# Attention layers on Trainium2: a third buffer for residual rows, weight loads spread over the steps, mask copies placed first

## The chip, the cores and the metric

The kernel runs on one NeuronCore of a Trainium2 chip. The metric is the device time of one execution, in microseconds (us). Three runs of the kernel before took 1181.93, 1186.46 and 1187.51 us; their median is 1186.46. One further execution was recorded by the hardware profiler; its durations are the ones used below. Engine names are those of the profile: PE is TensorE (matmuls), DVE is VectorE, ACT is ScalarE, POOL is GpSimd, SP is SyncE, which here only issues DMAs. A line L540 is line 540 of the kernel before.

## The reference

Four layers run one after the other on a bf16 input x of 2048 rows by 576 columns: A, B, A, B. Each adds its result to x, and each works on the LayerNorm of x.

```python
def _A_ref(x, wqkv, wo):          # H = 32, Dh = 18, W = 8, dil = 2
    qkv = transpose((x @ wqkv).reshape(B, S, 3, H, Dh), 2, 0, 3, 1, 4)
    q, k, v = (qkv[0], qkv[1], qkv[2])
    idx = arange(S)[:, None] - (arange(W) * dil)[None, :]
    ...
    logits = einsum('bhsd,bhswd->bhsw', q, kg) * Dh ** (-0.5)   # kg, vg: rows idx of k and v
    attn = softmax(where(idx >= 0, logits, -1e9))
    o = einsum('bhsw,bhswd->bhsd', attn, vg)
    return transpose(o, 0, 2, 1, 3).reshape(B, S, D) @ wo

def _B_ref(x, w_in, w_sp, b_sp, w_out):   # F = 4608, Fh = 2304
    z = gelu(einsum('bsd,df->bsf', x, w_in))
    z1, z2 = z[..., :Fh], layernorm(z[..., Fh:])
    g = einsum('ts,bsf->btf', w_sp, z2) + b_sp[None, :, None]
    return einsum('bsf,fd->bsd', z1 * g, w_out)

x = x + _A_ref(layernorm(x), ...); x = x + _B_ref(layernorm(x), ...)   # twice
```

So A is attention in which a row sees itself and seven earlier rows, two apart. B is a gated MLP whose gate mixes rows with a 2048 x 2048 matrix.

## The kernel before, in words

**Order of the work.** Layer A writes the order of its instructions out by hand for all engines (`tc.manual_schedule`): each engine runs its instructions in the order in which the program lists them, and waits where an operand is not ready. B does so for DVE and ACT in its first phase. SP and POOL also issue DMAs (L78); a DMA that must wait holds up whatever stands behind it on that engine.

**Layer A** (`layer_A`, L339) works on 17 tiles of rows in 34 steps, two steps per tile, one for each half of the heads. Step s holds the logits of step s+1 (`L_mm`, PE, L463), their exponential (`EXP`, ACT, L472), the product with v of step s (`PV`, PE L486, then the division into `o_t` on DVE, L492 and L493, and a transpose of `o_t` by DMA into `o_slot`), and then whatever `table[s]` lists. The table is filled with `at(step, function, ...)`:

- `PG` (L412): five matmuls (L428) project 512 columns of q or k into a PSUM bank; DVE (L397) or ACT copies them to a staging buffer `stg`; when both halves are staged, DMAs of 72 KB move each head's rows to their places in `QK`. These moves take the queues of their issuers in turn: `(sync, gpsimd)` by default, or `q2 = (gpsimd, sync, gpsimd)` (L561). Some PGs run ahead of step 0 (the list `pre`), others in steps 1 to 14.
- `VW`: the projection of v (L405).
- `O_CP`: DVE copies `o_slot` into the ring `oT` (L512). The last tiles are instead transposed by PE and copied by ACT (`O_T`, L518).
- `XO(i)` (L525): for even i, SP loads the residual rows i and i+1 of x into a buffer `xo` (288 KB in layer 0, 576 KB in layer 2; layer 0's are bf16, layer 2's float32). There are 2 such buffers.
- `WO(i, hh)` (L533): five matmuls (L540) of the output projection into a bank, and DVE adds `xo` to give `x_new` (L543). Row i's two halves stand at the steps `wo_steps[i]`: 8 and 9 for row 0, then about two steps later for each row, up to 34 and after for rows 14 and 15.
- `LN_STATS` (DVE statistics L234 and L236, POOL's reciprocal root L238 and L239), `LN_XN` (POOL, L259 and L262): the LayerNorm of `x_new` for layer B. `XST` and `XN_ST` store `x_new` and the normalised rows, `LN_T` loads the latter transposed into `xnT`, all through SP.

Ahead of step 0 in layer 0 stands a prologue: loads of x and weights, the LayerNorm of the 16 row tiles (`S_`, `R_`, `A_`, `T_`), the load of the mask pattern (`load_pat`), and `fill_window_rows(QK, 0)` (L194), which copies the mask rows into `QK` on DVE (L198 and L202) for one half of the columns. The heads' rows that the DMAs move land in the same tile `QK`, and the DMAs wait for these copies. In layer 2 the masks are copied after the first PGs, behind `setup_bufs` (DVE memsets of `P_sb` and `o_t`, L388 and L390) and the memset of `v_ext` (L687).

**Weights of the next layer.** B's z phase needs `win2a` (three chunks of 128 rows of `w_in`, loaded in 6 pieces of 288 KB) and `win2b` (6 pieces, into the room of the q/k weights). In layer 0 two of `win2a`'s three chunks are lent out as staging buffers until step 0's moves have gone; the third is not. For the second B layer `win2a` is loaded in the first one, by ACT (L1028); `win2b` is loaded in each A layer, by POOL.

**Layer B** (`layer_B`, L792) first makes z2 (z phase): groups of 8 units, each unit a PSUM bank of 128 x 512 (L851). ACT evicts them through GELU into `zp` (L898; 3 buffers, pool `p1`), DVE takes statistics (L900), DVE and POOL normalise into `Z`. Then come the gate (L975 for z1, L999 for the row mixing, the largest part) and the output (L1048, L1058).

**Pools.** A pool is a stretch of on-chip memory per partition, opened and closed with its layer. Layer A's small tiles (`x_new`, `xo`, `rec`, `ln_st`, `ln_mv`, `ln_rstd` and others) are in the pool `A{li}_sb` (L362). When a later pool takes the same bytes, the first instruction that writes a tile there waits for the last readers of the tiles that it covers (`reuse_waits="tile"`).

Of the kernel before, what the change touches and what calls it, by code (L numbers as in the profile page):

```python
# [13 lines left out]
bf16 = mybir.dt.bfloat16  # L14
# [4 lines left out]
P = 128  # L19
D = 576  # L20
# [43 lines left out]
class K:  # L64
# [274 lines left out]
    def layer_A(self, li):  # L339
        nc, tc, cfg = self.nc, self.tc, self.cfg  # L340
        S, NT, XW, NS = cfg.S, cfg.NT, cfg.XW, cfg.NS
        scale = float(DH ** -0.5)
        x_prev = self.A_x if li == 0 else self.xres[li - 1]
        x_prev_dt = bf16 if li == 0 else f32
# [6 lines left out]
        QK = main.tile([P, 2, 8, XW], bf16, name="QK")  # L351
# [10 lines left out]
        sb_cm = tc.tile_pool(name=f"A{li}_sb", bufs=2, reuse_waits="tile")  # L362
        sb = sb_cm.__enter__()
        x_news = [sb.tile([P, D], f32, name="x_new", tag="x_new", bufs=4) for k_ in range(4)]
        xos = {k_: sb.tile([P, 2, D], x_prev_dt, name="xo", tag="xo", bufs=2) for k_ in range(2)}
        if self.right is None:
            self.open_right()
        R = self.right
# [10 lines left out]
        def q0_(t):  # L379
            return cfg.tiles[t][0]  # L380
# [5 lines left out]
        def setup_bufs(eng):  # L386
            for pb in P_bufs:
                eng.memset(pb[:, :, :, QT:P], 1.0)  # L388
            for ob_ in o_bufs:
                eng.memset(ob_[:, D:640], 0.0)  # L390

        def exp_table():
            nc.scalar.activation(out=P_bufs[0][:, 0, 0, 0:1], in_=self.ones[:, 0:1], func=ACT.Exp)
# [130 lines left out]

        def XO(i):  # L525
            if i % 2 == 0:
                xo = xos.pop(i // 2, None) or sb.tile([P, 2, D], x_prev_dt, name="xo", tag="xo", bufs=2)
                src = self.rows_of(x_prev, i, 2) if li == 0 else x_prev[i * P:(i + 2) * P, :]
                self.dma(xo[:], src.rearrange("(a p) d -> p a d", p=P), eng=nc.sync)
                for k_ in range(2):  # L530
                    tails[i + k_] = dict(xo=xo[:, k_, :])
# [29 lines left out]
        q2 = (nc.gpsimd, nc.sync, nc.gpsimd)  # L561


        if li == 0:
# [32 lines left out]
            def S_(*tiles):  # L597
                for i in tiles:
                    st = sb.tile([P, 2, nc.vector.BN_STATS_DIM], f32, name="ln_st", tag="ln_st", bufs=3)
                    for s in range(2):  # L600
                        nc.vector.bn_stats(out=st[:, s, :], in_=xts[i][:, s * 288:(s + 1) * 288])
                    nc.vector.bn_aggr(out=mvs[:, i, :], in_=st[:])

            def R_(i0, n):
                rs = rstds[:, i0:i0 + n]
                nc.vector.tensor_scalar_add(out=rs, in0=mvs[:, i0:i0 + n, 1], scalar1=EPS)
                nc.gpsimd.tensor_tensor(out=rs, in0=rs, in1=self.neg_half[:, 0:1].to_broadcast([P, n]), op=ALU.pow)
            xns = {}

            def A_(*tiles):  # L610
                for i in tiles:
                    xns[i] = xn = self.xn_bufs[self.xn_rr % len(self.xn_bufs)]
                    self.xn_rr += 1
                    nc.vector.tensor_scalar(out=xn[:, 0:D], in0=xts[i], scalar1=mvs[:, i, 0:1],
                                            scalar2=rstds[:, i:i + 1], op0=ALU.subtract, op1=ALU.mult)
# [45 lines left out]
            self.load_pat(nc.sync)  # L661
            S_(9, 10, 11)
            R_(8, 4)
            S_(12)
            A_(8, 9, 10, 11)
            T_(8, 9, 10, 11)
# [14 lines left out]
        else:  # L681
            for k_, (d, cc) in enumerate([(d, cc) for d in range(5) for cc in range(2)]):
                for qk in ((1, 0) if d < 4 else (0,)):
                    PG(d, qk, cc, k_ == 0, (nc.gpsimd, nc.sync) if d == 0 else q2)
                if k_ == 0:
                    setup_bufs(nc.vector)
                    nc.vector.memset(v_ext[:, :, :, DH:DH + 1], 1.0)  # L687
                    self.fill_window_rows(QK, 0)
                    exp_table()
                if k_ == 1:  # L690
                    self.run_deferred()
                if k_ == 6:
                    self.fill_window_rows(QK, 1)
# [15 lines left out]
        def at(s, f, *a):  # L709
            table.setdefault(s, []).append((f, a))  # L710
        pgs = [(d, qk, cc) for d, cc in ((0, 2), (1, 2), (2, 2), (0, 3), (1, 3), (2, 3), (3, 2), (3, 3), (4, 2), (4, 3))
               for qk in ((1, 0) if d < 4 else (0,))]
        PG_END = 14
        pre, pgs = pgs[:6], pgs[6:]
        for k_, (d, qk, cc) in enumerate(pgs):
            at(1 + k_ if li == 0 else (k_ * PG_END) // len(pgs), PG, d, qk, cc, True)
        vws = [(t, hh) for t in range(nvw, NT) for hh in range(2)]
        if li == 0:
            at(0, VW, *vws[0], True)
# [10 lines left out]
        wo_steps = list(zip(units[0::2], units[1::2]))  # L730
        assert len(wo_steps) == NS
        for t in range(NT - 2):
            s = wo_steps[q0_(t) // P][0] - 1
            if t < NT - 3 and not in_ring(t):
                at(min(2 * t + 6, s), O_CP, t)
        for i in range(NS):
            s, s1 = wo_steps[i]
            if i % 2 == 0:
                at(max(s - 4, wo_steps[i - 3][1] + 1) if i >= 4 else s - 5, XO, i)
            at(s, WO, i, 0)  # L740
            at(s1, WO, i, 1)
            at(s1, LN_STATS, i)
            at(s1 + 1, LN_XN, i)
            at(s1 + 1, XST, i)
            if i < NS - 1:
                at(s1 + 4, XN_ST, i)
            if NS // 2 <= i < NS - 1:
                for k_ in range(2):
                    at(max(s1 + 6, NST + 3 * (i - NS // 2) - 4), LN_T, 2 * i - NS + k_)
        at(2 * (NT - 3) + 3, O_CP, NT - 3)  # L750
        if li == 0:
            at(0, self.load_wo, nc.sync)
            seen = sb.tile([P, 1], bf16, name="x_seen", tag="x_seen", bufs=1)
            at(0, lambda: nc.gpsimd.tensor_copy(out=seen[:], in_=self.xnT[:, 0, S - 1:S]))
            for f in reversed(self.load_win2a(nc.gpsimd)):
                at(0, f)
        at(PG_END + 1, alloc_win2b)
        for k_ in range(6):
            at(PG_END + 1 + k_, win2b_piece, k_)
        at(NST - 2, O_T, NT - 2)  # L760
        at(NST, O_T, NT - 1)
        for k_, (d, qk, cc) in enumerate(pre):
# [398 lines left out]
```

## Time and profile before

| what | value |
|---|---|
| median of three runs | 1186.46 us |
| the profiled execution: its own time | 1186.85 us |
| its span in the profile | 1185.1 us |
| PE busy | 1158.1 us, 98% |
| DVE, ACT, POOL busy | 47%, 29%, 24% |
| mean granted PE clock | 0.992 |
| layer 0 ends and its z phase starts at about | 134 us |
| layer 2 starts at about | 600 us, its z phase at 718 us |

"Busy" is the time in which an engine had an instruction running; PE's matmuls overlap, so a busy PE need not be at its peak. The granted clock is the share of full speed that the throttle left PE. A time line gives the start, the duration, the engine, line and operation, and in square brackets the idle time ahead of it with the instruction that released it. The chain of waits follows the work that ended last back from one instruction to what released it. For a DMA, "landing" is the time from its issue to its arrival.

### The profile page before, as it was taken

The numbers are of one execution on the slowest core, as the hardware profiler recorded it, in microseconds if no ns is written. First come the engines' busy times: TensorE is split into PE (matmuls) and PEld (weight loads), VectorE is DVE, ScalarE is ACT, GpSimd is POOL, SyncE is SP. The second block draws the span as 40 slices with busy tenths as digits, with TensorE's granted clock in tenths as the row PEclk, the third lists the DMA queues.
The fourth block names the chain that finished last, engine by engine and source line by source line (L and its number), as shares of the span: only waits on it lengthen the run. The fifth ranks groups of instructions, "written<-read, shape, count | busy, mean of one in ns | idle before, by whom it ended". The sixth has DMA issues, their size and how long they took to land.

```text
span 1185.1 us, 20051 instructions
## 1 busy us (share of the span) xinstructions
PE 1158.1 (98%) x8258; PEld 613.4 (52%) x8258; DVE 552.3 (47%) x1137; ACT 338.3 (29%) x491; POOL 280.9 (24%) x412
## 2 busy tenths in 40 slices
PE   9979899999999999999999998999999999999998
PEld 5547444444444444457755664444444444444677
DVE  8758688422233332245555785873232233232322
ACT  5559455111100111102147883550111110111000
POOL 3749855100000000001144796550000000000000
PEclk9989999999999999999999998999999999999999
DMA  8889796000000000049536798920000000001332
GB/s 194 186 145 252 191 210 142 23 12 12 12 1 12 12 12 1 18 142 283 170 85 122 190 257 198 230 67 13 12 12 12 12 1 12 12 1 37 116 106 73
DMA packets 182801, 106.44 MB, mean 90 GB/s; under 512 B 134939, under 2 KB 164043, under 8 KB 182710
## 3 DMA queue, kind: packets, MB, share of 16 engines
q1 hardware_dynamic: 170117, 84.54, 30.3%
q0 software_dynamic: 6240, 14.88, 4.7%
q10 hardware_dynamic: 6352, 5.75, 1.6%
q8 instruction: 64, 1.05, 0.4%
q14 instruction: 28, 0.22, 0.1%
HBM read 42.40 MB, written 21.77 MB: 54 GB/s over the span
## 4 chain that ended last, share of the span: by engine, by line
PE 90%; DMA 4%; DVE 3%; POOL 1%; ACT 1%; issue 1%; SPq 0%; DVEq 0%; POOLq 0%; ACTq 0%
PE pg L999 42%; PE po L1048 12%; PE pz L851 6%; PE pz L975 6%; PE pz1s L975 6%; PE pzs L851 6%; PE pp L428 4%; PE pv L405 2%; PE pw L540 2%; PE O_ps L486 2%; PE L_ps L463 1%; DMA QK<-stg 1%; DMA xo<-xres 1%; POOL QK L78 1%; ACT P_sb L472 1%
## 5 line engine op out<-in xcount | busy, mean ns | idle before, releaser
L999 PE MATMUL pg<-Wq,Z 128*128 128x512 bf16 x2304 | 500.2, 379 | 0.0
L999 PEld LDWEIGHTS <-Z 128*128 128x128 bf16 x2304 | 225.4, 98 | 271.8
L1003 DVE TENSOR_TENSOR g_tmp<-pg,ln_xn 128x512 f32<-128x512 f32 x144 | 99.6, 692 | 421.6 <-PE pg L999 421.6
L994 ACT ACTIVATE z1T<-pz 128x1024 bf16<-128x1024 f32 x36 | 34.9, 1020 | 500.2 <-PE pz L975 500.2
L78 POOL DMA_DIRECT2D wout<-in_B_w_out_dram x4 | 4.3, 1080 | 598.8 <-PE pg L999 598.8
L1048 PE MATMUL po<-wout,Z 128*128 128x288 bf16 x1152 | 141.4, 286 | 0.0
L472 ACT ACTIVATE P_sb<-L_ps 128x1440 bf16<-128x1440 f32 (+3 forms) x136 | 125.0, 972 | 36.8 <-PE L_ps L463 35.6
L1048 PEld LDWEIGHTS <-Z 128*128 128x128 bf16 x1152 | 112.7, 98 | 28.8
L851 PEld LDWEIGHTS <-xnT 128*128 128x128 bf16 (+1 forms) x800 | 68.9, 98 | 77.2 <-issue 12.5
L1004 DVE TENSOR_TENSOR Z<-g_tmp,z1T 128x512 bf16<-128x512 f32 x144 | 99.7, 692 | 12.2
L900 DVE BATCH_NORM_STATS2 z_st<-zp 128x6 f32<-128x512 bf16 (+1 forms) x160 | 91.7, 618 | 27.9 <-ACT zp L898 27.7
L975 PEld LDWEIGHTS <-w 128*128 128x128 bf16 (+1 forms) x640 | 53.7, 97 | 74.0 <-issue 13.6
L428 PE MATMUL pp<-xnT,wqk_sb 128*128 128x512 bf16 x360 | 83.6, 382 | 1.1 <-DVE o_t L493 1.1
L259 POOL TENSOR_SCALAR ln_xn<-x_new,ln_mv,ln_rstd 128x576 bf16<-128x576 f32 x32 | 74.1, 2314 | 2.3
L1058 DVE TENSOR_TENSOR x_new<-po,xo 128x288 f32<-128x288 f32 (+1 forms) x64 | 28.8, 455 | 87.4 <-PE po L1048 83.2
L975 PE MATMUL pz<-xnT,w 128*128 128x512 bf16 (+1 forms) x320 | 66.5, 380 | 0.0
L975 PE MATMUL pz1s<-xnT,w 128*128 128x512 bf16 (+1 forms) x320 | 66.5, 379 | 0.0
L540 PE MATMUL pw<-wo_sb,oT 128*128 128x288 bf16 x320 | 50.6, 296 | 13.9 <-DVE x_new L543 12.6
L851 PE MATMUL pz<-win2a,xnT 128*128 128x512 bf16 (+1 forms) x240 | 61.3, 367 | 0.0
L851 PE MATMUL pzs<-win2a,xnT 128*128 128x512 bf16 (+1 forms) x240 | 59.5, 358 | 0.0
L78 POOL DMA_DIRECT2D QK<-stg x80 | 48.6, 611 | 39.8 <-DVE stg L397 15.8
L898 ACT ACTIVATE zp<-pz 128x1024 bf16<-128x1024 f32 (+2 forms) x56 | 36.6, 720 | 74.4 <-PE pz L851 74.4
(108 smaller groups left out, 941.7 us busy)
## 6 DMA issues: line engine op xcount, KB each, us to landing
xres<-x_new SPq DMA_DIRECT2D x48, 288.0 KB
xo<-xres SPq DMA_DIRECT2D x32, 288.0 KB
wout<-in_B_w_out_dram POOLq DMA_DIRECT2D x4, 1296.0 KB, 7.5
xn_rows<-ln_xn SPq DMA_DIRECT2D x32, 160.0 KB
xo<-xres SPq DMA_DIRECT2D x8, 576.0 KB
w<-in_B_w_in_dram SPq DMA_DIRECT2D x16, 256.0 KB
QK<-stg POOLq DMA_DIRECT2D x52, 72.0 KB, 4.9
QK<-stg SPq DMA_DIRECT2D x42, 72.0 KB
```

What stands on the lines that cost most here:

```text
L78: return eng.dma_start(out=out, in_=in_)
L259: e.tensor_scalar(out=xn[:nrows, 0:D], in0=x_t[:nrows, :], scalar1=mv[:nrows, 0:1], scalar2=rstd[:nrows, 0:1], op0=ALU.subtract, op1=ALU.mult)
L428: nc.tensor.matmul(pp[:, :], lhsT=w, rhs=self.xnT[:, c, cc * 512:(cc + 1) * 512], start=(c == 0), stop=(c == 4))
L472: nc.scalar.activation(out=P_bufs[2 * jp + s % 2][:nk, :, :, 0:nq], in_=Lv[:nk, :, :, 0:nq], func=ACT.Exp, scale=scale)
L540: nc.tensor.matmul(pw[:, 0:288], lhsT=oT[:, c, r0:r0 + P], rhs=wo_sb[:, c, hh * 288:(hh + 1) * 288], start=(c == 0), stop=(c == 4))
L851: nc.tensor.matmul(out[:, o0:o0 + n], lhsT=self.xnT[r0:r1, c, r * P:(r + 1) * P], rhs=win2(c)[r0:r1, w0:w0 + n], start=start, stop=stop, t ...
L900: nc.vector.bn_stats(out=st[:, x // 512, :], in_=zp[:, x:x + min(512, w0 + n - x)])
L975: nc.tensor.matmul(outs[a_], lhsT=w1[r0:r1, c, sub * P:(sub + 1) * P], rhs=self.xnT[r0:r1, c, q * 512:(q + 1) * 512], start=start, stop=st ...
L999: nc.tensor.matmul(pg[:, :], lhsT=Z[:, jj, i, sub * P:(sub + 1) * P], rhs=Wq[q][:, i, :], start=(i == 0), stop=(i == NS - 1))
L1003: nc.vector.tensor_tensor(out=tmp[:], in0=pg[:, :], in1=bsp[:, qs], op=ALU.add)
L1004: nc.vector.tensor_tensor(out=uT(jj)[:, sub, qs], in0=tmp[:], in1=z1Ts[jj, sub][:, qs], op=ALU.mult)
L1048: nc.tensor.matmul(acc[hh], lhsT=u_rows(j, i), rhs=wouts[j // NJH][:, j % NJH, hh * 288:(hh + 1) * 288], start=(j == 0), stop=(j == NJ - 1))
```

## The change

- **Residual rows.** `xo` gets 3 buffers instead of 2 in both A layers, and the loads go out earlier. For i = 0, 2, ... 14 they stood at steps 3, 7, 12, 16, 19, 23, 27, 31 and now stand at 2, 6, 10, 12, 16, 20, 24, 27.
- **z weights.** All six pieces of `win2a` went out on POOL at step 0 of layer 0, behind a small copy (`x_seen`) that waited for the last transposed row. Now the two pieces of the chunk that is not lent go out on POOL in the prologue, after the statistics of row tiles 8 to 11; the other four go out at steps 13 to 16, by POOL and SP in turn. `x_seen` is gone.
- **win2b.** Its six pieces stood at steps 15 to 20 of both A layers and now stand at 17, 19, 21, 23, 25 and 27.
- **Moves.** In layer 0 the PGs of steps 1 to 8 use `q2`. With the order of the others this gives POOL 6, 5 and 5 of each group of eight moves and SP 2, 3 and 3, where each had 4.
- **Masks.** In layer 2 `fill_window_rows(QK, 0)` stands ahead of the memsets.

```diff
-        xos = {k_: sb.tile([P, 2, D], x_prev_dt, name="xo", tag="xo", bufs=2) for k_ in range(2)}
+        xos = {k_: sb.tile([P, 2, D], x_prev_dt, name="xo", tag="xo", bufs=3) for k_ in range(3)}
...
-                xo = xos.pop(i // 2, None) or sb.tile([P, 2, D], x_prev_dt, name="xo", tag="xo", bufs=2)
+                xo = xos.pop(i // 2, None) or sb.tile([P, 2, D], x_prev_dt, name="xo", tag="xo", bufs=3)
...
             R_(8, 4)
+            for f in self.load_win2a(nc.gpsimd)[4:6]:
+                f()
             S_(12)
...
                 if k_ == 0:
+                    self.fill_window_rows(QK, 0)
                     setup_bufs(nc.vector)
                     nc.vector.memset(v_ext[:, :, :, DH:DH + 1], 1.0)
-                    self.fill_window_rows(QK, 0)
                     exp_table()
...
-            at(1 + k_ if li == 0 else (k_ * PG_END) // len(pgs), PG, d, qk, cc, True)
+            at(1 + k_ if li == 0 else (k_ * PG_END) // len(pgs), PG, d, qk, cc, True, *((q2,) if li == 0 and k_ < 8 else ()))
...
-                at(max(s - 4, wo_steps[i - 3][1] + 1) if i >= 4 else s - 5, XO, i)
+                at(max(s - 7, wo_steps[i - 5][1] + 1) if i >= 6 else s - 6, XO, i)
...
-            seen = sb.tile([P, 1], bf16, name="x_seen", tag="x_seen", bufs=1)
-            at(0, lambda: nc.gpsimd.tensor_copy(out=seen[:], in_=self.xnT[:, 0, S - 1:S]))
-            for f in reversed(self.load_win2a(nc.gpsimd)):
-                at(0, f)
-        at(PG_END + 1, alloc_win2b)
+            for k_ in range(4):
+                at(PG_END - 1 + k_, self.load_win2a((nc.gpsimd, nc.sync)[k_ % 2])[k_])
+        s_b = PG_END + 3
+        at(s_b, alloc_win2b)
         for k_ in range(6):
-            at(PG_END + 1 + k_, win2b_piece, k_)
+            at(s_b + 2 * k_, win2b_piece, k_)
```

In the built program the third buffer moves the end of layer A's small pool. Before, it ended at byte 189,380 of a partition in layer 0 and 187,300 in layer 2, and the first buffer of `zp` in the next layer B began at 190,976. Now it ends at 191,652 and 191,908, so that some of its last tiles (`rec`, `ln_st`, `ln_mv`, `ln_rstd` among them) share bytes with that buffer.

## The prediction

> **What bounds it now.** I read the busy table, the chain of waits and the groups by cost, then the time line where TensorE (PE) idles.
>
> ```profile
> PE 1158.1 (98%) x8258; PEld 613.4 (52%) x8258; DVE 552.3 (47%) x1137; ACT 338.3 (29%) x491; POOL 280.9 (24%) x412
> L540 PE MATMUL pw<-wo_sb,oT 128*128 128x288 bf16 x320 | 50.6, 296 | 13.9 <-DVE x_new L543 12.6
> ```
>
> PE is busy 98%, so only its holes and its half-clock time can be won. The largest holes have one line, 12.6 us ahead of the output projection (L540), where PE waits for a bank that DVE's residual add (L543) must empty. I follow three of them and the start of layer 2.
>
> **Hole 1, layer 0, 72–77 us.** The chain from 45 to 85 us (start, us, what):
>
> ```profile
> 56.34 9.87 DMA QK<-stg
> ...
> 66.27 9.99 DMA o_slot<-o_t
> ...
> 77.05 1.36 PE pw L540 x5
> ```
>
> Two transfers of 10 us in a row end in PE's 4.03 us wait at 77.05. Why so slow? DMAs issued from 49 to 60 us (x, KB each, median us to landing):
>
> ```profile
> win2a<-in_B_w_in_dram POOLq DMA_DIRECT2D x6, 288.0 KB, 10.7
> QK<-stg POOLq DMA_DIRECT2D x5, 72.0 KB, 9.4
> ```
>
> From 26 to 45 us, with no win2a under way, the same QK moves land in 3.8 us. The queues' packets take 97% of the 16 DMA engines' time in the first window (65.5% on POOL's queue, 31.7% on SP's), 62% in the second. The wait also costs clock (window, PE busy, PEld, DVE, ACT, POOL, PE clock granted, DMA, GB/s):
>
> ```profile
> 72.00:76.00 4.00, 1.02 (x5) 0.28 (x3) 0.00 (x0) 1.36 (x2) 0.00 (x0) 0.84 1.16 137
> 76.00:80.00 4.00, 2.96 (x39) 1.71 (x40) 3.61 (x11) 0.97 (x1) 1.37 (x3) 0.50 0.49 127
> ```
>
> Before the wait the clock was 1.00, after it 0.50. In the chain, a projection and a step take 5.21 us from 77.05 to 82.26; the next step takes .32+.50+1.09+.61 = 2.52 and a projection .61, so 2.08 us are lost. With the waits of 1.08 (63.34), 1.31 (67.81) and 4.03, the hole is 8.5 us.
>
> **Hole 2, the end of layer 0.** PE's time line, then POOL's:
>
> ```profile
> 132.13 1.98 PE L540 MATMUL pw<-wo_sb,oT 128*128 128x288 bf16 x10 [3.13 <-DVE x_new L543]
> ```
>
> ```profile
> 140.89 2.30 POOL L259 TENSOR_SCALAR ln_xn<-x_new,ln_mv,ln_rstd 128x576 bf16<-128x576 f32 x1
> ```
>
> PE waits 3.13 us for row 14's add, and that for xo, loaded late (126.36, landing 5.18 us). Then ten matmuls take 1.98 us, not 1.24, and the first 16 of z (L851) 4.54, not 3.45: 1.84 of half clock. By oT's copy (129.03+.66) row 15 could start at 129.75. POOL (GpSimd) has no idle from 79.47 on and ends its last LayerNorm row (L259) at 143.19.
>
> **Hole 3, the start of layer 2**, in the chain:
>
> ```profile
> 603.70 1.85 issue
> 605.55 0.51 DVE v_ext L687
> ...
> 619.36 4.96 DMA QK<-stg
> ```
>
> The mask copies (L198) start at 605.69, behind memsets that wait 2.16 us for a transfer (xres<-x_new) and 1.85 more. They release POOL's QK moves, the last of which PE waits for (0.73+0.58, resuming at 624.59).
>
> **Hole 4, the end of layer 2**: chain, then POOL.
>
> ```profile
> 709.48 5.32 DMA xo<-xres
> ...
> 715.43 2.56 PE pw L540 x10
> ```
>
> ```profile
> 716.87 0.23 POOL L238 TENSOR_SCALAR ln_rstd<-ln_mv 128x1 f32<-128x1 f32 x1 [3.69 <-DVE ln_mv L236]
> ...
> 723.89 2.30 POOL L259 TENSOR_SCALAR ln_xn<-x_new,ln_mv,ln_rstd 128x576 bf16<-128x576 f32 x1
> ```
>
> Here PE waits 5.07; row 15 could start at 711.1. Half clock costs 2.3 (2.56 for 1.23, 4.44 for 3.45). POOL's last row ends at 726.19, its one idle time being those 3.69 us.
>
> **The change, part by part.**
>
> *z weights out of the burst.* Two of six pieces (0.59 MB) move to the prologue, four (1.18 MB) to steps 13 to 16, far from their first use at 134. With landings back at 3.8, the six q/k moves that POOL now issues one after the other (54.9 to 58.4, 0.6 each) land by about 63.3, when the stage is wanted (63.5); o_slot's transpose follows in time. So 8.0 of 8.5 us go; 0.5 stays for the moves shifted from SP to POOL. From below: if landings only fall to 7, some 3 us go. I take 8.0, since 3.8 is the row without the weights. On SP the shift of moves (two or three of eight, not four) leaves its transposes fewer moves to stand behind; on POOL it is up to two issues of 0.6 per group of eight, in steps where POOL otherwise waits for DVE's casts.
>
> The two early pieces start at 21.7 us beside the mask pattern's load. Each byte there could hold back the pattern; bounds 0 and 3.6 (10.7 x 2/6). I take 0.2, since queues at 26 to 45 us land in 3.8. Of the four later pieces two are issued by POOL, which has no idle there, so +1.3 on its chain (0.66 each), and two by SP, ahead of a store and a transpose that nobody waits for within a step. Their buffers were last read as staging before step 1, so they add no wait. The removed copy x_seen saves POOL a wait only.
>
> *win2b later and wider apart*: the same six issues, still on POOL; the last goes out at step 27, about 110 us, and is needed at 134 (18 us less 8.0 and a landing of 10.7 at worst). 0; without that cover z would wait 1 us per us.
>
> *Three xo buffers.* Loads go out 1 to 4 steps earlier (row 14's at step 27, not 31: some 9 us against a landing of 5.2). Each is placed one step after the add that frees its buffer, so SP, with its stores and transposes queued behind, waits for a step at most. The waits of holes 2 and 4 then go, and layer 2's small ones at 677 to 682 (1.1).
>
> *Masks first.* The copies can begin at 601.07, when DVE's last staging cast ends, not 605.69: PE could resume 4.6 earlier, but is itself ready only at 622.44 (+0.33 for the products): 624.59 becomes 622.77, 1.8 us. From below 0; memsets and v_ext are late next, but their reader comes after 622.
>
> **What is late next, and why the sum is small.** The third buffer takes 2,304 bytes per partition in layer 0, 4,608 in layer 2. As laid out, layer A's small pool ended 1,596 bytes below the first zp buffer of the following layer B; now it reaches into it, and the changed program's first GELU of each B (L898) waits for POOL's last LN_XN (row 15) and DVE's statistics; before, it waited for PE alone. Queued behind that GELU are all of ACT's evictions; PE can fill its 8 banks (one group, 8.0 us) and then stands.
>
> Layer 0: POOL's chain shifts by 8.0 and carries 1.3 more: 143.19 − 8.0 + 1.3 = 136.5. PE's group 0 is done at 129.75 − 8.0 − 0.15 + 1.24 + 8.0 = 130.8. One eviction later (1.02, from L994's 1020 ns) group 1 starts at 137.6; before, 143.19. 5.6 won, less 2.1 for a new half-clock stretch (PE idle 6.7; the three traced ones cost 1.84 to 2.3): 3.5. The Trainium skill, "TensorE: Matmul & The Clock Gate", Part 1, gives a busy window of about 3.4 us to get the clock back, so an estimate of 1.7 lost per restart; it also says that it takes 3.4 us of idle to lose it, and here 3.13 sufficed. By it the sum would be 0.8 better.
>
> Layer 2: POOL's last row ends at 726.19 − 3.69 − 1.8 = 720.7; group 0 at 711.1 − 1.8 − 1.1 + 1.23 + 8.0 = 717.4; group 1 starts at 721.8, before 726.98: 5.2 − 2.1 = 3.1. The 1.8 and 1.1 are inside it.
>
> **Sum**: 3.5 + 3.1 − 0.2 = 6.4. The profiled execution took 1186.85 (span 1185.1 and 1.75 around it): 1180.45. The median of the runs shown is 0.39 lower, 1186.46, so 1180.1.
>
> **Rivals.** *A, the forecast*, 1180; own range 1173 to 1185: down if POOL's chains are 2 us shorter (4 us, 2.1 of clock in layer 2, whose idle is then 2.4, and 1 of clock loss and prologue), up by landings and prologue. Chance 0.60. *B, hole 1 mostly stays*: the moves' own bytes and the output's transposes, not the weights, fill the DMA engines. Only 3 of the 8.5 us go: POOL ends at 143.19 − 3 + 1.3 = 141.5, group 1 starts at 142.6, 0.6 won less 2.1, so layer 0 gives −1.5, layer 2 keeps 3.1: about 1185. For it: the 97%, of which SP's third is not weights. Against it: 3.8 at 26 to 45. 0.15. The Trainium skill, "DMA: Bandwidth & Descriptors", section "Issuing engines are not separate DMA queues", says that DMAs of all engines run on the same 16 and interleave, so that another issuing engine saves issue time alone; by it the new split of the moves does nothing for their landing, and if only the split mattered, B would be the result. *C, the GELU's wait does not bind*: POOL is faster than assumed, or the buffers do not clash. Then every hole closes: 8.0 + 2.4 + 1.8 (layer 0) + 1.8 + 1.1 + 4.3 + 2.3 (layer 2) − 0.2 = 21.5: 1165. For it only that POOL's rows could speed up beside a less busy DVE; against it POOL's unbroken row of 3.55 us per LN. 0.10. *D, slower: the prologue.* The two early pieces delay the mask pattern, so the mask copies, the QK moves and the first logits; from 6.4 us of delay it eats the whole forecast, 1 us per us. At the burst's landing of 10.7 against 3.8 the pattern comes 7 late, PE loses the clock (2.1), and B's weaker gain holds: 1186.5 + 7 + 2.1 − 3 = 1192.6. For it: the pattern and its copies lie right behind those pieces; against: POOL's and SP's queues share little there. 0.15. Nothing else in the trace of before tells the price of this place.
>
> **Numbers.** Likeliest A: 1180.1. Out of the range I leave C (0.10) and half of D (0.07): 1173 to 1190. A measurement tells about 0.5% (5.9 us) from no change; the line for faster lies at 1180.5, in the middle of A. So faster: 0.35 of A and C's 0.10 = 0.45; same: 0.25 of A, B, and 0.07 of D = 0.47; slower (over 1192.4): the rest of D, 0.08.
>
> **What would show it.** Right: QK moves at 49 to 60 us land below 5 and PE has no wait above 1 at 72 to 77; pw (L540) no longer waits for x_new at the layers' ends; instead z (L851) or pzs stands 4 to 7 us for ACT's zp, that behind POOL's L259; masks start near 601. Wrong: if PE runs through both layer ends (C); if waits stay at 63 to 77 (B); if the first logits come later than now (D).

## The result, and the profile after

The changed kernel takes 1183.72 us (median of 22 runs, 1179.96 to 1188.26) against 1186.99 for the kernel before (22 runs, 1181.93 to 1190.64). The ratio is 0.9974, 95% interval 0.9963 to 0.9985: 3.1 us faster, where 6.4 were forecast. The profiled execution of the changed kernel is one of its shortest: 1180.51 us, span 1178.7.

Its page: PE's row, and the groups that answer to the large hole of before. The lines of the changed kernel's second layer type stand one further down (L852 is L851 of before, L899 is L898).

```profile
PE 1155.2 (98%) x8258; PEld 611.9 (52%) x8258; DVE 552.0 (47%) x1137; ACT 338.5 (29%) x491; POOL 281.8 (24%) x413
...
L852 PE MATMUL pz<-win2a,xnT 128*128 128x512 bf16 (+1 forms) x240 | 61.8, 369 | 7.8 <-ACT zp L899 7.8
```

PE's waits in total (us in all, times, longest):

```profile
PE pz L852 <- ACT zp L899: 7.8, 2, 5.4
PE O_ps L486 <- DVE o_t L493: 3.3, 5, 1.7
PE L_ps L463 <- ACT P_sb L472: 2.5, 6, 0.5
PE pw L540 <- ACT oT L520: 1.5, 2, 0.8
PE pw L540 <- DVE x_new L543: 1.4, 2, 0.9
```

The 12.6 us ahead of the output projection (L540) are 1.4. In their place stand 7.8 us ahead of the z phase (L852), in two waits, which the kernel before did not have.

**Hole 1** is gone. DMAs issued from 49 to 60 us:

```profile
QK<-stg POOLq DMA_DIRECT2D x9, 72.0 KB, 5.6
QK<-stg SPq DMA_DIRECT2D x4, 72.0 KB
```

The moves land in 5.6 us instead of 9.4, a little slower than the 3.8 that the forecast took, and between 55 and 85 us PE waits nowhere over 0.3 us.

**The end of layer 0**, the chain from 115 to 142 us:

```profile
133.88 2.31 POOL ln_xn L259
136.19 0.02 issue
136.21 1.03 ACT zp L899
137.25 0.04 issue
137.29 4.85 PE pz L852 x11
```

POOL's last LayerNorm row ends at 136.19, the first GELU follows at once, and only then does PE go on, at 137.29 after 5.37 us of idle. At full clock these 11 matmuls would have taken some 2.4 us (16 took 3.45 at 143.19 before); here they take 4.85, at half clock, and the view ends before the clock is back. From the start of this group to the first matmul of the row mixing (L999 of before) PE takes 74.7 us, where it took 71.9 before, so the lost clock cost 2.8. This is the stretch around it (window, PE, PEld, DVE, ACT, POOL, clock, DMA, GB/s):

```profile
135.00:145.00 10.00, 7.71 (x29) 2.97 (x28) 5.97 (x11) 4.46 (x9) 3.97 (x5) 0.66 0.68 122
```

**The start of layer 2**, in the chain, has no wait left for masks or moves:

```profile
595.24 19.43 PE pp L428 x90
614.67 4.90 PE pv L405 x40
619.57 0.34 PE L_ps L463 x16
619.90 6.15 PE pp L428 x28
```

**The end of layer 2**, the chain again:

```profile
716.95 2.31 POOL ln_xn L259
719.27 1.03 ACT zp L899
...
720.35 3.61 PE pz L852 x16
```

The same wait for POOL, but of 2.42 us, and 16 matmuls behind it take 3.61 (3.45 at full clock): here the clock was kept, the granted clock being 1.00 throughout.

### The profile page after: what moved, and what is told of

The parts are those of the page before. It is cut to its first block, busy times and chain, and to the rows that moved or that the text cites. A ratio compares the mean times of both kernels' runs of the same rounds, so it can differ in the third digit from the quotient of the medians.

```text
span 1178.7 us, 20062 instructions
## 1 busy us (share of the span) xinstructions
PE 1155.2 (98%) x8258; PEld 611.9 (52%) x8258; DVE 552.0 (47%) x1137; ACT 338.5 (29%) x491; POOL 281.8 (24%) x413
## 4 chain that ended last, share of the span: by engine, by line
PE 91%; POOL 3%; DVE 2%; DMA 2%; ACT 1%; issue 0%; SPq 0%; DVEq 0%; POOLq 0%; ACTq 0%
PE pg L1000 42%; PE po L1049 12%; PE pp L428 6%; PE pz L976 6%; PE pz1s L976 6%; PE pz L852 6%; PE pzs L852 5%; PE pv L405 2%; POOL ln_xn L259 2%; PE O_ps L486 2%; PE pw L540 2%; DMA o_slot<-o_t 2%; PE L_ps L463 1%; DMA QK<-stg 1%; POOL ln_rstd L239 0%
## 5 line engine op out<-in xcount | busy, mean ns | idle before, releaser
L852 PEld LDWEIGHTS <-xnT 128*128 128x128 bf16 (+1 forms) x800 | 69.0, 98 | 85.4 <-issue 21.8
L428 PE MATMUL pp<-xnT,wqk_sb 128*128 128x512 bf16 x360 | 82.6, 379 | 0.0
L852 PE MATMUL pz<-win2a,xnT 128*128 128x512 bf16 (+1 forms) x240 | 61.8, 369 | 7.8 <-ACT zp L899 7.8
L78 POOL DMA_DIRECT2D QK<-stg x84 | 51.3, 614 | 39.6 <-DVE stg L397 26.2
L852 PE MATMUL pzs<-win2a,xnT 128*128 128x512 bf16 (+1 forms) x240 | 59.5, 358 | 0.0
L925 POOL TENSOR_SCALAR Z<-zp,z_mv,z_rstd 128x256 bf16<-128x256 bf16 x32 | 54.5, 1704 | 3.3
L899 ACT ACTIVATE zp<-pz 128x1024 bf16<-128x1024 f32 (+2 forms) x56 | 36.6, 720 | 64.1 <-PE pz L852 53.7
```

Of the source, the lines that this page charges most:

```text
L78: return eng.dma_start(out=out, in_=in_)
L428: nc.tensor.matmul(pp[:, :], lhsT=w, rhs=self.xnT[:, c, cc * 512:(cc + 1) * 512], start=(c == 0), stop=(c == 4))
L852: nc.tensor.matmul(out[:, o0:o0 + n], lhsT=self.xnT[r0:r1, c, r * P:(r + 1) * P], rhs=win2(c)[r0:r1, w0:w0 + n], start=start, stop=stop, t ...
L925: eng.tensor_scalar(out=Z[:, b0:b1, i, :], in0=zv[:, b0:b1, :], scalar1=mv[:, 0:1], scalar2=rstd[:, 0:1], op0=ALU.subtract, op1=ALU.mult)
```

## The experiments

Ratios are to the kernel before, run on the same chip; gains in us are worked out from the ratio and the median of before. Line numbers shift by a few where a kernel adds lines.

**1. Is it the shared bytes?** `small_first` is the changed kernel with layer A's small tiles placed low, so that the shared bytes belong to an `xo` buffer that is read for the last time some rows before the end:

```diff
+        small = [sb.tile([P, 16], f32, name="rec", tag="rec", bufs=2),
+                 sb.tile([P, 2, nc.vector.BN_STATS_DIM], f32, name="ln_st", tag="ln_st", bufs=3),
+                 sb.tile([P, 2], f32, name="ln_mv", tag="ln_mv", bufs=3),
+                 sb.tile([P, 1], f32, name="ln_rstd", tag="ln_rstd", bufs=3)]
         x_news = [sb.tile([P, D], f32, name="x_new", tag="x_new", bufs=4) for k_ in range(4)]
```

> The changed kernel, with layer A's small statistics tiles (rec, ln_st, ln_mv, ln_rstd) allocated ahead of x_new and xo, so that the bytes shared with the next layer's first zp buffer belong to an xo buffer last read rows earlier. Theory: the two waits of z's matmuls for ACT's zp (5.4 + 2.4 us in the profile of the changed kernel), and 2 to 4 us of half clock behind them, vanish; time 1171 to 1175 against some 1184 for the changed kernel. Rival: something else holds the z phase (POOL's LayerNorm itself, the transposed loads): the waits come back under another name and the time stays at 1182 to 1185.

Measured: 1172.05 us (5 runs, 1170.19 to 1174.05), ratio 0.989 (0.9874 to 0.9907): 13.0 us faster than before, and 11.6 faster than the changed kernel (1183.63, experiment 4), from which it differs in four allocations alone. PE's largest waits now:

```profile
PE L_ps L467 <- ACT P_sb L476: 2.5, 6, 0.5
PE O_ps L490 <- DVE o_t L497: 2.1, 4, 1.0
PE pw L544 <- DMA oT<-o_t: 1.7, 1, 1.7
PE pw L544 <- ACT oT L524: 1.5, 2, 0.8
```

No wait for ACT's zp (pz) is left. The theory holds; this is the fastest version of the study.

**2. The shared bytes alone.** `pad_before` is the kernel before with an unused tile in the third buffer's place.

```diff
+        pad = sb.tile([P, 2, D], x_prev_dt, name="pad", tag="pad", bufs=1)
```

> The kernel before, with an unused tile of 2,304 bytes (layer 0) or 4,608 bytes (layer 2) behind the two xo buffers: only the shared bytes, no third buffer. Theory: the first GELU of each B now waits for POOL's last LayerNorm, which ends at 143.19 and 726.19 in the trace of before, where group 1 of z starts at 143.19 and 726.98 anyway: +1.1 and +0.3 us, so about 1.4 us slower than before (0.1%). Rival: the shared bytes cost by themselves what the changed kernel misses (7 us or more slower), or nothing at all.

Measured: 1188.93 us (10 runs), ratio 1.003 (1.0015 to 1.0045): 3.6 us slower, more than the 1.4 expected and far less than 7. PE's wait at the end of layer 0:

```profile
144.78 1.40 PE L852 MATMUL pz<-win2a,xnT 128*128 128x512 bf16 x3 [2.46 <-ACT zp L899]
```

Before, the group behind this point started with no wait. So the same bytes cost 3.6 us in the kernel before, where PE itself comes late, and 11.6 in the changed kernel (experiment 1).

**3. The change without its third buffer.** `two_xo`:

```diff
-bufs=3) for k_ in range(3)}
+bufs=2) for k_ in range(2)}
...
-                at(max(s - 7, wo_steps[i - 5][1] + 1) if i >= 6 else s - 6, XO, i)
+                at(max(s - 4, wo_steps[i - 3][1] + 1) if i >= 4 else s - 5, XO, i)
```

> The changed kernel with two xo buffers and the loads at their old steps; the other parts stay. Theory: no shared bytes; the burst's hole in layer 0 (8.0) and the late start of layer 2 (1.8) are gone, the waits for late residual rows at both layer ends stay: about 1177, some 6 us faster than the changed kernel. Rival: the third buffer is what gains, and without it the time is 1184 or more.

Measured: 1177.96 us (6 runs), ratio 0.9938 (0.9922 to 0.9954). As expected: without the buffer that was to remove the waits at the layers' ends the kernel is faster. Those waits are back (2.81 and 2.04 us in its trace), and they are shorter than the ones for zp (5.37 and 2.42). It is still 5.9 us slower than `small_first`, so the third buffer with its earlier loads does gain once its bytes lie elsewhere.

**4. The changed kernel again**, `after_again`, beside these.

> The changed kernel once more, beside the others. Theory: 1182 to 1185, with one or two stretches of half clock: behind the first wait for zp always, behind the second (2.4 us in the profile) in some executions only. Rival: the clock is alike in all executions and the spread comes from transfers.

Measured: 1183.63 us (12 runs), ratio 0.9987 (0.9976 to 0.9999). Its profile took 1183.15, a median run. Layer 0 is as in the first profile, layer 2 is not. POOL's waits for DVE's statistics there:

```profile
672.50 0.23 POOL L238 TENSOR_SCALAR ln_rstd<-ln_mv 128x1 f32<-128x1 f32 x1 [1.62 <-DVE ln_mv L236]
706.67 0.23 POOL L238 TENSOR_SCALAR ln_rstd<-ln_mv 128x1 f32<-128x1 f32 x1 [1.51 <-DVE ln_mv L236]
```

and PE's wait for zp:

```profile
721.50 1.44 PE L852 MATMUL pz<-win2a,xnT 128*128 128x512 bf16 x3 [2.45 <-ACT zp L899]
722.74 0.63 PE L852 MATMUL pz<-win2b,xnT 128*128 128x512 bf16 x1
```

Three matmuls take 1.44 us, not 0.81, and the next 0.63, not 0.38: behind 2.45 us of idle the clock was lost, which it was not behind 2.42 in the first profile.

**5. Masks alone, weights alone.** `masks_only` and `weights_only` are the kernel before with one part each (the move of `fill_window_rows`; the move of the six `win2a` pieces and nothing else).

> The kernel before with the mask copies of layer 2 ahead of the memsets, nothing else. Theory: 1.8 us at the start of layer 2 (PE's waits of 0.73 and 0.58 for QK go), but the end of that layer still waits for late residual rows, so the 1.8 come through whole: about 1185. Rival: the residual load at the end is late by the clock and not by the layer's start, so that nothing comes through: 1187.

> The kernel before with the z weights moved (two pieces in the prologue, four at steps 13 to 16, no x_seen copy), nothing else. Theory: the hole of 8.5 us in layer 0 goes, and layer B's first group does not wait for POOL: about 1178.5 to 1180. Rival 1: the new split of the moves is needed as well, and some 3 us stay: 1182. Rival 2: the pieces in the prologue delay the mask rows: 1185 or more.

Measured: masks 1183.91 us (12 runs), ratio 0.9978 (0.9964 to 0.9992), 2.6 us for an expected 1.8. Weights 1184.12 us (12 runs), ratio 0.9982 (0.9966 to 0.9998): 2.1 us, where 7 to 8.5 were expected. That is a miss. PE's time line in layer 0 shows why:

```profile
95.43 0.79 PE L540 MATMUL pw<-wo_sb,oT 128*128 128x288 bf16 x5 [1.22 <-DMA oT<-o_t]
99.54 0.77 PE L540 MATMUL pw<-wo_sb,oT 128*128 128x288 bf16 x5 [1.89 <-DVE x_new L543]
103.06 1.36 PE L540 MATMUL pw<-wo_sb,oT 128*128 128x288 bf16 x5 [0.52 <-DVE x_new L543]
```

The hole at 63 to 82 us is gone, and a smaller one, the matmuls from 100 to 107 at half clock, stands at 95 to 103: the four late pieces at steps 13 to 16 met `win2b` at steps 15 to 20. The burst was moved, not dissolved (experiment 6 tests this). The profile is that of the slowest of the 12 runs (1188.38 us), and its first attention product came at 51.1 us, 3.0 later than before. By itself it would also fit the rival of a slower prologue.

**6. Weights and win2b together.** `weights_win2b` adds to `weights_only` the wider spacing of `win2b`.

```diff
-        at(PG_END + 1, alloc_win2b)
+        s_b = PG_END + 3
+        at(s_b, alloc_win2b)
...
-            at(PG_END + 1 + k_, win2b_piece, k_)
+            at(s_b + 2 * k_, win2b_piece, k_)
```

> The kernel before with the z weights moved, as in weights_only, and win2b at every second step from 17 on in both layers; nothing else. Theory: weights_only gained only 2.2 us because its four late pieces met win2b at steps 15 to 20 (PE waits of 1.22, 1.89 and 0.52 at 95 to 103 and a half clock behind them); spread, the burst is gone and some 6 to 8 us are won: 1178.5 to 1180.5. Rival: win2b costs nothing there, and the split of the moves or the run's prologue made the difference: 1183 to 1185.

Measured: 1177.85 us (6 runs), ratio 0.9935 (0.9911 to 0.9958): 7.7 us, against 2.1 without the spacing. The two intervals do not touch, and both kernels have the same prologue, so the prologue is not what held `weights_only` back. Not all of this is the burst of layer 0: layer 2, which the weights do not enter, takes 197.1 us up to its row mixing here, 200.3 in `weights_only` and 200.7 before (one profile each), so the spacing seems to gain there too.

**7. win2b of layer 2 back** to steps 15 to 20, in the changed kernel: `win2b_back_l2`.

> The changed kernel with the six win2b pieces of layer 2 back at steps 15 to 20 (layer 0 as changed). Theory: in layer 2 the pieces that now go out at steps 21 to 27 share the DMA engines with the output's transposes, whose copies wait 2.9 to 4.0 us for them (0.2 before); so PE and POOL reach the end of layer 2 some 2 us later than forecast. Put back, these waits fall under 1 us and the time falls by 1.5 to 3 us, to 1180.5 to 1182. Rival: the earlier xo loads, which stand right ahead of those transposes, delay them; then the waits stay and so does the time, 1183 to 1185.

Measured: 1185.78 us (12 runs), ratio 0.9986 (0.9970 to 1.0002). Not faster; the theory that the late pieces of `win2b` delay the transposes falls. PE's largest wait there:

```profile
683.40 1.36 PE L540 MATMUL pw<-wo_sb,oT 128*128 128x288 bf16 x5 [4.41 <-DVE x_new L543]
```

DVE's copy of `o_slot` had waited 5.18 us for its transpose. Crowded earlier, the transposes are late earlier.

**8. The residual loads one step later**, behind a transpose instead of ahead of one: `after_xo_odd`, and `small_xo_odd` on top of `small_first`.

```diff
-                at(max(s - 7, wo_steps[i - 5][1] + 1) if i >= 6 else s - 6, XO, i)
+                at((max(s - 7, wo_steps[i - 5][1] + 1) if i >= 6 else s - 6) | (i >= 4), XO, i)
```

> The changed kernel, its xo loads from row 4 on one step later where that step is even (11, 13, 17, 21, 25, 27), so that SP issues each behind the output's transpose of that step and not right ahead of the next one. Theory: in layer 2 the load of 576 KB right ahead of a transpose makes DVE's copies of o_slot wait (2.9 to 4.0 us in two profiles of the changed kernel) and POOL run dry (1.1 and 3.1 us); turned round, both fall under 1 us, layer 2 ends 1.5 to 3 us earlier and the time is 1181 to 1182.5. Rival: the transposes are late because the DMA engines are full (94 to 96% in those stretches), whatever the order: 1183 to 1185.

> The same later xo loads, in the kernel with the small tiles first (1172.05). Theory of the order: 1169.5 to 1171. Rival of the full engines: 1171.5 to 1173.5.

Measured: 1183.68 us (12 runs), ratio 0.9978 (0.9962 to 0.9994), and 1174.21 (4 runs), ratio 0.9908 (0.988 to 0.9936). No gain; DVE's waits for `o_slot` are 3.5 and 2.9 us. The order beside the transposes is not it.

**9. The loads at their old steps, three buffers kept**: `after_xo_old_steps`.

> The changed kernel with three xo buffers and the loads at the steps of before. Theory: in layer 2 DVE's copies of o_slot wait at most 1.5 us for their transposes (2.9 to 4.0 in the changed kernel, 1.5 with two buffers and old steps); the waits for late residual rows at both layer ends come back (2 to 5 us), and the wait for zp behind them shrinks by as much, since POOL ends as before: 1183 to 1186 in all. Rival: the transposes wait 2.9 us or more here too, so that the loads' time does not matter to them.

Measured: 1183.90 us (10 runs), ratio 0.9985 (0.9964 to 1.0007), as expected. DVE's waits for DMAs in layer 2:

```profile
692.09 0.42 DVE L512 COPY oT<-o_slot 128x440 bf16<-128x440 bf16 x2 [0.45 <-DMA o_slot<-o_t]
699.64 0.35 DVE L512 COPY oT<-o_slot 128x600 bf16<-128x600 bf16 x1 [0.67 <-DMA o_slot<-o_t]
708.09 0.82 DVE L543 TENSOR_TENSOR x_new<-pw,xo 128x288 f32<-128x288 f32 x2 [3.35 <-DMA xo<-xres]
```

The transposes come almost in time (1.1 us in all), and the last residual rows are late again. PE waits 2.80 and 3.91 us for `x_new` and then 2.61 us and nothing for zp: one wait takes the other's place, at the same time in sum.

**10. The new split of the moves, and the early pieces**, each undone in `small_first`: `small_no_split` lets the moves of steps 1 to 8 take SP and POOL in turn again; `small_late6` issues the two early pieces at steps 17 and 18.

> The changed kernel with the small tiles first (1172.05) and without the new split of the moves in layer 0. Theory, and the rule that issuers share the same DMA engines: the same time within 1 us, 1171 to 1173. Rival: SP's transposes stand behind more moves and PE waits again at 60 to 80 us: 1174 or more.

> The kernel with the small tiles first, and the two early z-weight pieces at steps 17 and 18 as well, none in the prologue. Theory: the prologue cost next to nothing (first attention products at 46.8 to 48.4 us in profiles with the pieces, 47.4 to 48.6 without), so 1171 to 1174, a little slower if the late pieces crowd the output's transposes. Rival: the pieces do delay the mask rows, as in two profiles with 50.6 and 51.1: 1169 to 1171.

Measured: 1175.17 us (5 runs), ratio 0.9904 (0.9885 to 0.9923), and 1174.94 (5 runs), ratio 0.9901 (0.9878 to 0.9925). Both intervals overlap that of `small_first` (0.9874 to 0.9907); neither part is shown to gain or to lose. 1175.17 lies where the rival of `small_no_split` had put it, but not for its reason: PE waits nowhere over 0.2 us at 60 to 80 us in its trace. And `small_late6`, with no weight load in the prologue, reached its first attention product at 50.2 us, about as late as `small_no_split` (50.6) and `weights_only` (51.1), which have the two pieces there: the lateness comes without the pieces too.

**11. Two more profiles of the changed kernel.**

> The changed kernel, a third profile. Theory: the stage from the start of layer 2 to its gate takes 197 us where the clock is kept behind the second wait for zp and 200 to 201 where it is lost, and POOL waits 1 to 3 us for rows in layer 2 in either. Rival: the stage's length goes with POOL's waits alone, whatever the clock.

> The changed kernel, a fourth profile. The same as for the third.

Measured: 1182.51 and 1182.07 us. They are in this table, whose columns are read from PE's and POOL's time lines (us; gates 1 and 2 are the first row-mixing matmuls, L999 of before, of the two layers B; layer 2 starts with its first projection, L428; "rows" is from the start of POOL's first to that of its last LayerNorm row in layer 2, "dry" is POOL's wait for DVE's statistics between them):

| kernel | first O_ps (L486) | gate 1 starts | layer 2 starts to gate 2 | rows | dry | waits for zp | span |
|---|---|---|---|---|---|---|---|
| before | 48.1 | 215.0 | 200.7 | 63.1 | 3.7 | none | 1185.1 |
| changed, profile 1 | 47.3 | 212.0 | 197.2 | 60.9 | 1.1 | 5.37, 2.42 | 1178.7 |
| changed, 2 | 46.8 | 211.1 | 200.8 | 63.0 | 3.1 | 5.96, 2.45 | 1181.4 |
| changed, 3 | 48.5 | 213.4 | 197.8 | 61.5 | 1.6 | 5.41, 1.64 | 1180.7 |
| changed, 4 | 47.6 | 212.6 | 198.1 | 61.8 | 2.0 | 6.03, 1.79 | 1180.3 |
| small_first | 48.0 | 205.8 | 195.0 | 61.2 | 1.4 | none | 1170.3 |
| weights_win2b | 47.5 | 205.8 | 197.1 | 61.7 | 1.7 | none | 1172.7 |

Where the clock was kept behind the wait for zp in layer 2 (profiles 1, 3 and 4) the stage takes 197 to 198 us, where it was lost (2) 200.8. Against profile 1 that is 3.6, of which the clock is some 1.5 (group 1 of z to gate 2 takes 73.4 us, 71.9 in the others) and POOL's lateness 2.1.

In profiles 3 and 4 the clock had been lost earlier in layer 2, behind waits of 2.80 and 1.87 us for DVE's `o_t` (profile 3, then 4; window, PE, PEld, DVE, ACT, POOL, clock, DMA, GB/s):

```profile
707.00:710.00 3.00, 2.98 (x14) 1.56 (x13) 2.75 (x9) 0.00 (x0) 2.59 (x3) 0.50 0.57 167
```

```profile
705.50:708.50 3.00, 3.00 (x19) 1.92 (x17) 2.08 (x8) 0.00 (x0) 1.52 (x3) 0.50 0.85 259
```

That loss did not reach the sum, since PE afterwards stood 1.64 and 1.79 us for POOL's last row all the same.

## Why the prediction was right in kind and too large

**Right: the mechanism.** The third buffer's bytes make layer B's first GELU wait for POOL's last row. POOL was to end at 136.5 in layer 0 and ended at 136.19 in profile 1; PE was to go on at 137.6 and went on at 137.29, 137.50, 139.57 and 139.36 in the four profiles; the idle time was to be 6.7 and is 5.4 to 6.0. The half clock behind it was to cost 2.1 and cost 2.8, 1.6, 1.9 and 1.3 (from the start of that group to gate 1, against 71.9 us before): a fair mean, but no constant. Taking the wait away gave 1172.05, and the case without it had been put at 1165. That case was rightly given a small chance.

**Right: hole 1 and the masks.** The moves' landing fell from 9.4 to 5.6, PE's waits at 63 to 77 are gone, and the chain of layer 2 has no wait for masks. POOL's first LayerNorm row in layer 0 starts 8.8, 8.7, 6.5 and 6.7 us earlier, where 8.0 were booked. From there its rows take 60.8 to 60.9 us, 59.0 before: 1.8 more, not 1.3. Layer 0 was to win 3.3; gate 1 starts 3.0, 3.9, 1.6 and 2.3 us earlier in four profiles, 2.7 in the mean. Up to 0.6 of that is luck of the prologue: its first product came 0.6 earlier in the mean and had been booked as 0.2 later.

**The step that failed: "POOL's last row ends at 726.19 − 3.69 − 1.8".** I took it that POOL, which had only one idle time in layer 2, would run through once that was gone. Its rows, first to last, were then to take 63.1 − 3.7 = 59.4 us. They take 60.9, 63.0, 61.5 and 61.8: POOL runs dry for 1.1 to 3.1 us, since DVE's statistics come late. Counted from the start of layer 2, its last row ends 1.5, 3.6, 2.1 and 2.4 us later than forecast, 2.4 in the mean. The chain of profile 2 shows what the statistics wait for:

```profile
698.24 5.49 DMA o_slot<-o_t
703.78 0.04 issue
703.83 0.35 DVE oT L512
...
705.19 0.74 DVE ln_st L234 x2
...
706.37 0.22 DVE ln_mv L236
706.59 0.08 issue
706.67 0.23 POOL ln_rstd L238
```

DVE's total waits for these transposes around the end of layer 2, before, then in profiles 1 and 2:

```profile
DVE oT L512 <- DMA o_slot<-o_t: 0.2, 1, 0.2
```

```profile
DVE oT L512 <- DMA o_slot<-o_t: 2.9, 2, 1.6
DVE oT L512 <- DMA o_slot<-o_t: 4.0, 2, 2.2
```

The earlier loads of residual rows, free in my sum, are what changed: with them DVE waits 2.9 to 4.0 us for the output's transposes in layer 2, with the old steps 1.1 (experiment 9). There POOL runs dry all the same (2.7 us), now for the late rows. Moving a load behind a transpose does not help (8), nor does taking the `win2b` pieces out of that stretch (7). That the DMA engines are simply full there (SP's queue alone takes 94 to 96% of their time in the 32 us around the last transposes, before and after) fits all three, but was only argued. So layer 2, forecast at 3.1, gave 3.5, −0.1, 2.9 and 2.6, 2.2 in the mean.

**The clock in layer 2** I had charged with 2.1 in every run, behind a wait for zp of 4.3. That wait came out at 1.6 to 2.45, because PE was late as well: DVE, held up by the same transposes, kept it waiting 1.66, 1.88, 2.80 and 1.87 us for `o_t` near 705. Behind zp the clock was lost in one of four profiles, and in two it was lost earlier, where it cost nothing in the sum. This partly covered the first error, and it was luck: 2.4 us of lateness appear as 0.9 us of lost gain. The Trainium skill, "TensorE: Matmul & The Clock Gate", Part 1, describes a free-running window of activity, with a cost that varies from run to run; waits of 1.87 and 1.88 us with different outcomes (lost in profile 4, kept in profile 2) agree with that, while its figure of about 3.4 us of idle before the clock drops does not bound it from below: 1.87 sufficed here.

**What is left.** The four profiled executions took 1182.1 us in the mean, 4.8 less than the 1186.85 of before, so the two layers' shortfalls (0.6 and 0.9) are nearly all of the 1.6 that these profiles miss of the 6.4. The other 1.7, down to the measured 3.1, the profiles do not show: 34 timed runs of the changed kernel took about 1183.7. Their mean granted clock is 0.995, that of the four profiles 0.9965; over the 22 runs the time falls by 0.75 us per 0.001 of clock, which would make 1.1 of the 1.6 us between profiles and timed runs. That is a correlation; in which stage those runs lose it was not seen, and this part of the shortfall stays open.

**Wrong, though it did not show: "win2b later and wider apart: 0".** Alone the weights win 2.1 us, with `win2b` spread 7.7. The 8.0 that I booked on the weights need both parts (and some of the 7.7 comes from layer 2, experiment 6); I had asked whether `win2b` would arrive in time, and not what it would meet on the way.

**Rivals.** B (the hole stays) fell in the changed kernel, but is what `weights_only` shows at another place. D (the prologue) fell: the first product came at 46.8 to 48.5 us in four profiles of the changed kernel, at 48.1 before, and `small_late6` was late (50.2) without the early pieces. The rule that issuers share the DMA engines, by which the split of the moves wins nothing for their landing (the Trainium skill, "DMA: Bandwidth & Descriptors", "Issuing engines are not separate DMA queues"), is not contradicted: the runs without the split (1170.84 to 1177.40 us) and with it (1170.19 to 1174.05) overlap.

## What to carry to other kernels

A larger buffer can cost more at the pool boundary behind it than it wins in its loop: look at which tiles share bytes with the next stage's first writes, and give the shared end to a tile that dies early, which here cost nothing more than the order of four allocations. A transfer moved out of one burst must be followed to where it lands, against everything already issued there. And a queue of work that never idled is not proof that its feeder can go faster; when the one wait is taken out, look at what feeds it next.

## What the runs showed of the hardware

- The length of one wait did not decide whether PE kept its clock. Behind waits of 1.73 us (`small_first`, at 92 us) and 1.87 (profile 4, at 705) the granted clock fell to half; behind 1.88 (profile 2, at 705), 2.42 (profile 1, at 720) and 2.46 (`weights_win2b`, at 125) it did not.
- Each of the losses followed here lasted some 3.4 or 6.8 us by the granted clock: 6.8 in profile 1 from 136.2 to 143.0 us, 3.4 in profile 4 from 138.7 to 142.1. What it cost is about half of the time that PE worked within it: 5.7 us in profile 1, which lost 2.8, and 2.7 in profile 4, which lost 1.3, though profile 4 had idled longer before (6.03 us against 5.37).
- `weights_only` and `weights_win2b` are the same program up to step 15, yet their first attention product came at 51.1 and 47.5 us; a single profile does not tell a prologue's cost to better than these 3.6 us.
